# A fused attention, FFN and routed-expert kernel on one core: the two products of a Newton step on one pair of tiles, wider warm-up matmuls, and a new order of all engines up to the experts

## The chip, the cores and the metric

One NeuronCore of a Trainium2 chip runs the whole program in one launch. The metric is the device time of that launch in microseconds: lower is better. Below, TensorE (PE) is the matrix engine, VectorE (DVE), ScalarE (ACT) and GpSimd (POOL) are the elementwise engines, and SP is the queue that issues nearly all DMAs.

## The reference, cut to what matters

Three layers follow each other: Nyström attention over 4 batches, 8 heads, 576 positions and 64 dimensions; an FFN (512 to 2048 to 512) with elu on the 2304 tokens that result; and a layer of 8 experts of which each token takes two.

```python
q_lm, k_lm = means of q and k over 32 groups of 18 positions
A  = sm(q, k_lm)          # 576 x 32 for each batch and head; sm is a row softmax
Bm = sm(q_lm, k_lm)       # 32 x 32
C  = sm(q_lm, k)          # 32 x 576
Z = Bm.T / (norm1(Bm) * norminf(Bm) + 1e-06)
for _ in range(6):
    Z = 2 * Z - Z @ Bm @ Z
x = (A @ Z @ C @ v)       # heads side by side: 2304 x 512
h = x @ w_in
y = np.where(h > 0, h, np.exp(np.minimum(h, 0)) - 1) @ w_out
# routing: y @ w_gate + log1p(exp(y @ w_noise)) * noise, the two best of 8
# experts: out[tokens of e] += weight * (maximum(y @ w1[e], 0) @ w2[e])
```

## The kernel before, in words

**Attention**, one call of `attention(b)` for each batch. The 8 heads are two halves of four (`k.0`, `k.1`, `q.0`, `q.1`: loads of 0.59 MB). `lmmm` or `lmsum` sum the landmarks, by 9 products with an identity on TensorE (batch 0) or on VectorE or GpSimd (the others); `bmm` forms Bm's scores, `csmm` those of C, `asmm` those of A, and the functions beside them the softmaxes. The six Newton steps are written as R and Y: R begins as a difference from the identity, and each step squares it (`sqmm`, `sqout`) and adds the product of R and Y to Y (`umm`, `uout`). Each of these products is eight matmuls of 32 x 32 blocks in fp32, one for each head (`blocks`, L464). `sqout` copies R from PSUM on ScalarE, `uout` adds Y on VectorE. From Y, `cv` (the product of C with v), `zcv` and `zout` give Z, and `gmm` multiplies Z with the rows of w_in that belong to each head: that is G (512 columns for each call, four calls for a batch). So the FFN's first layer is one product of A with G.

**The FFN** runs over six chunks of tokens (512, 256, and four of 384) and 16 blocks of 128 hidden columns. For each, `l1` is the product of A and G, `X`, `T`, `S`, `H`, `O` are the steps of elu (`O` is the low half of the float16 pair, a subtraction on VectorE or GpSimd, by the letter behind the item), and `l2` adds the product with w_out's 16 pieces of 128 rows (`wout`). w_in's 16 pieces and w_out's 16 pieces arrive as 64-bit words and are put into floats first, by `I.j.0` to `I.j.3` and `Wa.k.0` to `Wa.k.3` (one on ScalarE, two on VectorE, one on GpSimd), and w_out is then split into a float16 pair (`Wb`).

**Routing and experts.** `RT` to `RS` choose the experts and write the rows; expert 0's steps and then experts 1 to 7 follow. The order of experts 1 to 7 is written in loops behind the table.

**What sets the order.** Nothing is scheduled by the compiler: `ORDER` is a string of items, and `do` calls for each item, in that order, the function that issues its instructions. Each engine then runs its own instructions in the order of the string, and SP its loads. An engine that stands in front of a wait stands with everything behind it. `0:sqmm.1` is step 1 of batch 0, `L2.3.5.1` block 5 of chunk 3 for its token tile 1, `wi.6` and `Wl.5` are loads of weight pieces, `F.16` is 16 warm-up matmuls (`warm`, L661), which compute nothing that is used. In batch 2 and 3 the products of both kinds, `pq` (R and R) and `pu` (R and Y), take turns in one PSUM bank ("n"), which is also that of chunk 0's fourth token tile. In batch 0 each has its part of a fixed bank.

Of the kernel before, what the change touches and what calls it, by code (L numbers as in the profile page):

```python
# [8 lines left out]
F32 = mybir.dt.float32  # L9
F16 = mybir.dt.float16  # L10
# [7 lines left out]
M = 32  # L18
# [38 lines left out]
I.3.0 I.6.3 I.4.1 Wa.0.1 0:asmm.0 F.16 F.16 I.4.2 Wl.5 I.2.3 I.5.1 0:xtl.1.1.0 0:astr.0 0:xth.1.1.1 0:lcp.0.A
0:xtl.1.1.1 wi.1 0:xtp.0.1.0 0:asmax.0 0:bmm I.5.2 Wl.1 0:csmm.0 I.4.3 0:bmax 0:xth.0.1.0 0:xtp.0.1.2 F.16 0:bex
0:csmax.0 wi.14 wi.7 I.3.3 0:assub.0.G 0:bnorm 0:nmm Wa.0.2 F.15 0:nval 0:csexp.0 Wa.1.0 Wa.5.0 Wb.4.0.V F.15
0:xth.1.1.2 Wa.1.1 0:sqmm.0 Wa.5.1 I.1.1 Wa.1.2 I.5.0 0:xtl.1.1.2 0:xtl.0.1.0 0:sqout.0 wi.10 0:xth.0.1.2 nz.3.1 Wa.5.2  # L60
0:y0 Wa.1.3 I.7.1 Wl.3 0:csmm.1 F.16 Wa.5.3 F.3 0:xtp.0.1.1 Wa.3.0 0:asexp.0 0:umm.0 0:sqmm.1 0:sqout.1 0:csmax.1
# [122 lines left out]
def attn_ffn_moe_kernel(ctx: ExitStack, tc: tile.TileContext, q: bass.AP, k: bass.AP, v: bass.AP,  # L184
# [1213 lines left out]
```

## Time and profile before

| | us |
|---|---|
| median of 3 runs | 792.57 |
| lowest and highest | 788.42, 794.16 |
| profiled execution, its own time | 790.42 |
| its span in the profile | 788.6 |

The span is what the views below divide. A view of stretches gives the busy time of each engine between two times; a timeline lists the instructions of one engine in order, with what it waited for ahead of each; groups by line sum the instructions of one source line. What the rows say, by the words of the profile: `L469` is line 469, `pq<-R` is a tile and what it is made from, `x16` the count of instructions or of instruction parts.

### The profile page before, as it was taken

The page shows a single profiled execution, that of the slowest core. Times are in us where ns is not written, and L with a number is a line of the kernel's source. Part 1 is how long each engine was busy: PE and PEld are TensorE (multiplying, and loading weights), DVE is VectorE, ACT ScalarE, POOL GpSimd, SP SyncE. Part 2 cuts the span into 40 slices and gives each one's busy share as a digit, 9 for nine tenths or more (in the row PEclk, how much of TensorE's full clock was granted, in tenths as well). Part 3 has the DMA queues.
Part 4 walks back from the last instruction along what each step waited for, and adds up shares of the span by engine and source line. Part 5 has one row for each costly group of instructions (what it writes and reads, how often), then busy time and mean ns, then how long its engine had stood idle before and what let it go on. Part 6 is the DMA issues. An engine that isn't in the chain of part 4 may idle for free. (4 is left out here: it accounts for less than half of the span.)

```text
span 788.6 us, 18639 instructions
## 1 busy us (share of the span) xinstructions
PE 762.4 (97%) x7517; PEld 454.8 (58%) x7518; DVE 623.5 (79%) x1366; ACT 426.9 (54%) x821; POOL 274.6 (35%) x303
## 2 busy tenths in 40 slices
PE   8878998999999999999999999999999999999997
PEld 8653444564544545665555775665747566574763
DVE  5969988797875777655737579989999998999951
ACT  3757776757556456446432365555636555564530
POOL 2434455636241332141403252333425132312222
PEclk9979999999999999999999999999999999999999
DMA  9977696286896221614242976474756647472381
GB/s 343 329 193 199 160 285 256 42 171 197 238 246 150 87 83 41 174 69 107 82 81 96 177 190 150 106 212 62 244 94 198 141 86 218 73 238 26 38 302 67
DMA packets 136205, 123.25 MB, mean 156 GB/s; under 512 B 102892, under 2 KB 105964, under 8 KB 136017
## 3 DMA queue, kind: packets, MB, share of 16 engines
q1 hardware_dynamic: 125392, 100.67, 45.6%
q0 software_dynamic: 10720, 21.34, 12.7%
q8 instruction: 60, 0.98, 0.5%
q14 instruction: 33, 0.26, 0.1%
HBM read 70.62 MB, written 39.76 MB: 140 GB/s over the span
## 5 line engine op out<-in xcount | busy, mean ns | idle before, releaser
L692 PE MATMUL y<-wout,g 128*128 128x512 f16 x864 | 208.2, 382 | 2.1 <-issue 1.9
L1135 PE MATMUL ey<-w,eh 128*128 128x512 f16 x768 | 167.2, 379 | 0.0
L1161 POOL DMA_INDIRECT acc<-eo,tk x35 | 73.8, 2108 | 207.6 <-ACT eo L219 78.8
L692 PEld LDWEIGHTS <-g 128*128 128x128 f16 x864 | 80.0, 98 | 92.5 <-issue 10.2
L1135 PEld LDWEIGHTS <-eh 128*128 128x128 f16 x768 | 75.0, 98 | 89.1
L654 PE MATMUL h<-AT,G 128*128 128x192 f16 (+3 forms) x768 | 108.7, 288 | 3.4 <-DVE e L680 3.3
L654 PEld LDWEIGHTS <-G 128*128 128x128 f16 x768 | 63.7, 98 | 46.4 <-issue 11.6
L685 POOL TENSOR_TENSOR g<-e,g 128x384 f16<-128x384 f32 (+2 forms) x45 | 43.9, 976 | 132.4 <-ACT g L219 114.7
L219 ACT ACTIVATE eh<-c 128x300 f16<-128x300 f32 x112 | 47.8, 453 | 65.1 <-DVE c L1057 57.2
L219 ACT ACTIVATE g<-e 128x384 f16<-128x384 f32 (+2 forms) x96 | 49.2, 520 | 48.2 <-DVE e L680 23.2
L219 ACT ACTIVATE e<-h 128x384 f32<-128x384 f32 (+2 forms) x96 | 46.3, 486 | 40.4 <-PE h L654 23.3
L680 DVE SCALAR_TENSOR_TENSOR e<-e,h 128x384 f32<-128x384 f32 (+2 forms) x96 | 51.3, 546 | 14.6 <-ACT e L219 12.5
L219 ACT ACTIVATE eo<-ey,ws 128x512 f32<-128x512 f32 (+3 forms) x60 | 32.4, 540 | 45.7 <-PE ey L1135 33.6
L877 POOL DMA_INDIRECT xs<-rows,pos x36 | 37.7, 1048 | 54.3 <-DVE mcum L861 26.4
L916 DVE SCALAR_TENSOR_TENSOR w<-ew,w 128x1024 f16<-128x1024 f32 x36 | 43.9, 1242 | 13.7 <-ACT w L219 11.9
L1040 PE MATMUL eb<-tx,wpC 128*128 128x300 f16 x336 | 47.4, 291 | 0.0
L1069 DVE SCALAR_TENSOR_TENSOR eh<-c,eh 128x300 f16<-128x300 f32 x112 | 46.0, 461 | 1.0 <-ACT eh L219 0.2
L685 DVE TENSOR_TENSOR g<-e,g 128x384 f16<-128x384 f32 (+2 forms) x51 | 29.4, 581 | 19.0 <-ACT g L219 18.8
L1057 DVE TENSOR_TENSOR c<-eb,u 128x300 f32<-128x300 f32 x84 | 36.6, 459 | 3.6 <-PE eb L1040 3.6
L1040 PEld LDWEIGHTS <-wpD 128*128 128x128 f16 x336 | 32.8, 98 | 11.4 <-issue 1.3
L1040 PEld LDWEIGHTS <-wpB 128*128 128x128 f16 x336 | 32.9, 98 | 10.0
L1040 PEld LDWEIGHTS <-wpC 128*128 128x128 f16 x336 | 32.7, 97 | 10.1
(256 smaller groups left out, 1379.7 us busy)
## 6 DMA issues: line engine op xcount, KB each, us to landing
ew<-in_moe_w_dram SPq DMA_DIRECT2D x64, 512.0 KB
wi<-in_moe_w_in_dram SPq DMA_DIRECT2D x16, 512.0 KB
wo<-in_moe_w_out_dram SPq DMA_DIRECT2D x16, 512.0 KB
k<-in_k_dram SPq DMA_DIRECT2D x8, 576.0 KB
q<-in_q_dram SPq DMA_DIRECT2D x8, 576.0 KB
v<-in_v_dram SPq DMA_DIRECT2D x4, 1152.0 KB
out_dram<-acc SPq DMA_DIRECT2D x1, 4608.0 KB
xs<-zrow SPq DMA_DIRECT2D x3, 1300.0 KB
```

The source lines that it names most:

```text
L219: return A.activation(o, i, f, **kw)
L654: T.matmul(p[:, c0:c0 + n], GT[b, f // 8][:, g, x, fs], AT[b][:, g, y, o:o + n], start=(i == 0), stop=(i == 5))
L680: V.scalar_tensor_tensor(x[1], x[1], x[2], x[0], op0=ALU.mult, op1=ALU.max)
L685: e.tensor_tensor(out=HT[c, f][:, 1], in0=x[1], in1=HT[c, f][:, 0], op=ALU.subtract)
L692: T.matmul(YP[c, t], h[:, x, 128 * t:128 * t + 128], WOUT[f][:, y], start=(f == 0 and i == 0), stop=(f == 15 and i == 2))
L877: n = nc.gpsimd.indirect_dma_start(out=xs[:, :], out_offset=bass.IndirectOffsetOnAxis(ap=R["pos"][:, i // 2, i % 2:i % 2 + 1], axis=0), in ...
L916: V.scalar_tensor_tensor(dst[1][:, ks, :], t, scale, dst[0][:, ks, :], op0=ALU.mult, op1=ALU.subtract)
L1040: T.matmul(p, w_op(e, w, s, k, f), x_op(e, x, t, k), start=(i == 0 and k == 0), stop=(i == 2 and k == 1))
L1057: V.tensor_tensor(out=o, in0=EB[n, f], in1=EU[a, f], op=ALU.add)
L1069: V.scalar_tensor_tensor(lo, o, 0.0, hi, op0=ALU.max, op1=ALU.subtract)
L1135: T.matmul(p, EH[e, f][:, x, 128 * j:128 * j + 128], W2T[e][y][:, f, :], start=start, stop=stop)
L1161: nc.gpsimd.indirect_dma_start(out=acc[:, :], out_offset=bass.IndirectOffsetOnAxis(ap=TK[e][:live(j), j:j + 1], axis=0), in_=EO[e, j], in_ ...
```

## The change

1. **Newton.** R and Y of a step stand side by side in one tile `R` of [128, 2, 2, 32] (head half, R or Y, columns). `nm(i)` multiplies R with [R|Y]: eight matmuls of 32 rows and 64 columns, whose result is the next R and the addend of the next Y. `sqmm` is left for the first step alone and `umm` for the last. A batch has 56 block matmuls in place of 96. `sqout(i + 1)` and `uout(i)` both read the result of `nm(i)`, and `nm(i + 1)` reads both of theirs.
2. **Warm-ups.** `warm` multiplies a tile of ones with itself up to four times side by side, so with up to 512 columns. 258 matmuls of 128 columns become 63 of at most 512 (239 times 128 columns).
3. **Names.** The big tiles of w_in, w_out and G are made by whichever of their parts the order names first, and so is C's row of sums.
4. **ORDER** is written anew up to the experts, SP's loads with it. 61 of the 96 `O` stand on GpSimd (45 before), 35 on VectorE (51 before); in chunk 0 VectorE has 3 of them (7 before). 60 `T` stand on ScalarE (56 before).

```diff
 ORDER = """
-wi.0 F.16 0:k.0 Wl.4 I.0.0 0:q.0 Wa.4.0 F.16 F.16 0:xtp.1.0.0 0:xtp.1.0.2 wi.2 I.0.1 0:xth.1.0.0 I.0.2 0:lmmm.1.0 Wa.4.1
+F.30 0:k.0 0:q.0 0:xtp.1.0.0 0:xtp.1.0.1 0:xth.1.0.1 Wl.4 0:xtp.1.0.2 0:xtp.0.0.1 0:q.1 0:xtp.0.0.2 0:lmmm.0.0
...
+    hot = cst.tile([128, 128], F16, name="hot")
+    V.memset(hot, 1.0)
...
-            if kk % 4 == 0:
-                t = half(f"wout{kk}").rearrange("p (k s f) -> p k s f", k=4, s=2)
+            if kk not in WOUT:
+                t = half(f"wout{kk // 4}").rearrange("p (k s f) -> p k s f", k=4, s=2)
...
+        def ry(i):
+            if i not in R:
+                R[i] = sa.tile([128, 2, 2, M], F32, tag="R", bufs=NR, name=f"R{b}{i}")
+            return R[i]
+
         def sqmm(i):
-            p = X["pq", i] = small(f"pq{b}{i}", n_tag, 0, 64).rearrange("p (g m) -> p g m", g=2)
-            x = X["BB"][:, 1] if i == 0 else R[i - 1]
-            blocks(p, x, x)
+            p = X["pq", 0] = small(f"pq{b}{i}", n_tag, 0, 64).rearrange("p (g m) -> p g m", g=2)
+            blocks(p, X["BB"][:, 1], X["BB"][:, 1])
+
+        def nm(i):
+            p = X["pq", i + 1] = small(f"pu{b}{i}", n_tag, 0, 128).rearrange("p (g s m) -> p g s m", g=2, s=2)
+            blocks(p, R[i][:, :, 0], R[i])
...
-                act(r, p)
+                act(r, p[:, :, 0])
...
         def umm(i):
             p = X["pu"] = small(f"pu{b}{i}", u_tag, 256, 64, "l1").rearrange("p (g m) -> p g m", g=2)
-            blocks(p, R[i], X["Y"])
+            blocks(p, R[i][:, :, 0], R[i][:, :, 1])

         def uout(i):
-            Y, X["Y"] = X["Y"], tile_a([128, 2, M], "Y", 2)
-            V.tensor_tensor(out=X["Y"], in0=X["pu"], in1=Y, op=ALU.add)
+            p, o = (X["pq", i + 1][:, :, 1], ry(i + 1)[:, :, 1]) if i < 5 else (X["pu"], tile_a([128, 2, M], "Y"))
+            V.tensor_tensor(out=o, in0=p, in1=R[i][:, :, 1], op=ALU.add)
+            X["Y"] = o
...
-        for _ in range(n):
-            T.matmul(WARM[0][:, :128], ident16, ident16, start=True, stop=True)
+        while n:
+            w = min(n, 4)
+            T.matmul(WARM[0][:, :128 * w], hot, hot[:, None, :].to_broadcast([128, w, 128]), start=True, stop=True)
+            n -= w
```

**SP's queue, the start of the program.** `k01` is k of batch 0, its second half; `wi` and `wo` are raw pieces of w_in and w_out, `noise_t` the routing's noise. Before:

```order
L1211 DMA wi00_114<-in_moe_w_in_dram 128x1024
L228 DMA k00_133<-in_k_dram 128x1152
L267 DMA wo4_135<-in_moe_w_out_dram 128x1024
L228 DMA q00_139<-in_q_dram 128x1152
L1211 DMA wi02_183<-in_moe_w_in_dram 128x1024
L228 DMA q01_212<-in_q_dram 128x1152
L1211 DMA wi12_216<-in_moe_w_in_dram 128x1024
L228 DMA k01_223<-in_k_dram 128x1152
```

And now:

```order
L226 DMA k00_125<-in_k_dram 128x1152
L226 DMA q00_127<-in_q_dram 128x1152
L267 DMA wo4_139<-in_moe_w_out_dram 128x1024
L226 DMA q01_149<-in_q_dram 128x1152
L737 DMA noise_t_97<-in_moe2_noise_dram 32x4x8
L226 DMA k01_187<-in_k_dram 128x1152
L1224 DMA wi01_212<-in_moe_w_in_dram 128x1024
L267 DMA wo5_218<-in_moe_w_out_dram 128x1024
```

k's second half is the sixth load in place of the eighth, behind two weight pieces fewer; `v0`, batch 0's v, is the 21st load in place of the 27th.

**TensorE, the Newton steps of batch 2.** `pu2i` and `pq2i` are the PSUM results of step i, `R2i` and `Y2` its operands, `y22` and `g2_f` result and left operand of the FFN's second layer, `pcv2` the product with v. Before:

```order
L469 MATMUL pu23_3509<-Y2_3416,R23_3468 32x32 x8
L692 LDWEIGHTS g2_8_3425
L692 MATMUL y22_3048<-wout8_1561,g2_8_3425 128x512
L692 LDWEIGHTS g2_8_3425
L692 MATMUL y22_3048<-wout8_1561,g2_8_3425 128x512
L692 LDWEIGHTS g2_8_3425
L692 MATMUL y22_3048<-wout8_1561,g2_8_3425 128x512
L469 MATMUL pq25_3523<-R24_3503 32x32 x8
```

And now:

```order
L469 MATMUL pu20_2950<-R20_2900 32x64 x8
L704 LDWEIGHTS g2_5_2731
L704 MATMUL y22_2740<-wout1_205,g2_5_2731 128x512
L704 LDWEIGHTS g2_5_2731
L704 MATMUL y22_2740<-wout1_205,g2_5_2731 128x512
L704 LDWEIGHTS g2_5_2731
L704 MATMUL y22_2740<-wout1_205,g2_5_2731 128x512
L469 MATMUL pu21_2969<-R21_2959 32x64 x8
L534 MATMUL pcv2_2980<-v2_1839,ET20_2860 32x64 x8
```

Two narrow groups, of R and Y and of R alone, stood for each step, with FFN products between them; now one group of 64 columns stands for each, which reads one tile, and between steps 0 and 1 lie three FFN products.

**GpSimd, chunk 0.** `g0_f` is the low half of the FFN's activations of chunk 0, `wo` and `wout` are w_out's pieces, `lmt211` and `k12` are the partial and the whole sum of batch 2's k, second half. Before:

```order
L685 TENSOR_TENSOR g0_10_1724<-e0_10_1683,g0_10_1724 128x512
L263 TENSOR_TENSOR wo10_1516<-wo10_1516 128x512
L263 TENSOR_TENSOR wo13_1461<-wo13_1461 128x512
L292 TENSOR_TENSOR wout12_1777<-wo12_1387,wout12_1777 128x512
L263 TENSOR_TENSOR wo11_1544<-wo11_1544 128x512
L292 TENSOR_TENSOR wout8_1561<-wo11_1544,wout8_1561 128x512
L685 TENSOR_TENSOR g0_12_1916<-e0_12_1843,g0_12_1916 128x512
```

And now:

```order
L697 TENSOR_TENSOR g0_11_1456<-e0_11_1358,g0_11_1456 128x512
L263 TENSOR_TENSOR wo11_1289<-wo11_1289 128x512
L697 TENSOR_TENSOR g0_10_1510<-e0_10_1379,g0_10_1510 128x512
L326 TENSOR_TENSOR lmt211_1595<-k21_1451 128x576
L328 TENSOR_TENSOR lmt211_1595<-lmt211_1595 128x256
L328 TENSOR_TENSOR lmt211_1595<-lmt211_1595 128x128
L328 TENSOR_TENSOR lmt211_1595<-lmt211_1595 128x64
L329 TENSOR_TENSOR k12_1592<-lmt211_1595 128x64
L292 TENSOR_TENSOR wout2_1278<-wo11_1289,wout2_1278 128x512
L263 TENSOR_TENSOR wo12_1389<-wo12_1389 128x512
L263 TENSOR_TENSOR wo13_1360<-wo13_1360 128x512
```

The sum of batch 2's k stands now between two subtractions of chunk 0 and the pieces 2, 12 and 13 of w_out; before it stood in chunk 1.

## Rows read from the trace of the kernel before

**Rows 1.** The page, busy time and instructions of each engine over the whole execution.

```profile
PE 762.4 (97%) x7517; PEld 454.8 (58%) x7518; DVE 623.5 (79%) x1366; ACT 426.9 (54%) x821; POOL 274.6 (35%) x303
```

**Rows 2.** Busy time in four stretches; the columns are named in its line.

```profile
core 0: us, PE busy (x) PEld busy (x) DVE busy (x) ACT busy (x) POOL busy (x), PEclk, DMA share, GB/s
0.00:58.10 58.10, 46.20 (x820) 39.69 (x822) 41.83 (x114) 31.27 (x67) 20.50 (x25) 0.91 0.88 293
58.10:140.00 81.90, 76.49 (x780) 32.85 (x777) 74.38 (x144) 60.31 (x118) 42.07 (x40) 0.96 0.71 217
140.00:406.40 266.40, 263.39 (x2603) 141.61 (x2596) 187.67 (x520) 150.37 (x331) 91.48 (x129) 1.00 0.49 129
406.40:788.60 382.20, 376.35 (x3327) 240.67 (x3325) 319.58 (x592) 184.94 (x307) 120.56 (x111) 1.00 0.59 142
```

**Rows 3.** TensorE's timeline, prologue; start, us, engine line op, [idle before <- releaser].

```profile
16.46 2.27 PE L336 MATMUL l1b<-k,ident 128*128 128x128 f32 x18 [0.77 <-DMA k<-in_k_dram]
...
24.48 0.27 PE L430 MATMUL nb<-lT 64*32 64x32 f16 x15
...
29.66 0.33 PE L469 MATMUL nb<-BB 32*32 32x32 f32 x16
...
43.90 0.18 PE L469 MATMUL l1b<-Y,R 32*32 32x32 f32 x1 [2.63 <-issue]
...
46.32 2.79 PE L524 MATMUL pcv<-v,ET 96*32 96x64 f32 x96 [1.36 <-DMA v<-in_v_dram]
...
51.36 0.70 PE L558 MATMUL l1b<-Yd,CV 128*64 128x64 f32 x8
51.99 2.53 PE L666 MATMUL warm<-ident 128*128 128x128 f16 x22
...
56.10 2.18 PE L666 MATMUL warm<-ident 128*128 128x128 f16 x36
58.12 3.18 PE L654 MATMUL h<-AT,G 128*128 128x512 f16 x12
61.23 1.09 PE L621 MATMUL pg<-win,Z 64*32 64x512 f32 x16
```

**Rows 4.** ScalarE's timeline, first loaded weight piece (same columns).

```profile
5.00 0.68 ACT L219 ACTIVATE wi<-wi 128x512 int32<-128x512 uint32 x1 [2.86 <-DMA wi<-in_moe_w_in_dram]
```

**Rows 5.** Busy time in the first 30 us (columns as in rows 2).

```profile
0.00:30.00 30.00, 25.55 (x353) 24.22 (x355) 20.48 (x64) 15.03 (x32) 8.51 (x14) 1.00 0.93 341
```

**Rows 6.** Groups by line, whole execution: busy us, mean ns | idle before.

```profile
L685 POOL TENSOR_TENSOR g<-e,g 128x384 f16<-128x384 f32 (+2 forms) x45 | 43.9, 976 | 132.4 <-ACT g L219 114.7 <-DVE sm L446 9.3 <-DVE ax L572 5.3
...
L685 DVE TENSOR_TENSOR g<-e,g 128x384 f16<-128x384 f32 (+2 forms) x51 | 29.4, 581 | 19.0 <-ACT g L219 18.8
...
L323 DVE TENSOR_REDUCE k<-q 128x64 f32<-128x1152 f32 x5 | 10.7, 2144 | 0.0
...
L219 ACT ACTIVATE ET<-pe 96x512 f32<-96x512 f32 x12 | 6.9, 581 | 1.1 <-PE pe L511 1.1
...
L219 ACT ACTIVATE ax<-ax 128x576 f32<-128x576 f32 x8 | 5.4, 678 | 0.0
```

**Rows 7.** ScalarE's timeline, two copies of a Newton step, batch 0.

```profile
33.73 0.22 ACT L219 ACTIVATE R<-nb 128x64 f32<-128x64 f32 x1 [1.35 <-PE nb L469]
34.40 0.22 ACT L219 ACTIVATE R<-nb 128x64 f32<-128x64 f32 x1 [0.45 <-PE nb L469]
```

**Rows 8.** TensorE's timeline in batch 2's Newton steps and its product with v.

```profile
203.14 2.76 PE L692 MATMUL y<-wout,g 128*128 128x512 f16 x12
205.84 0.33 PE L469 MATMUL pq<-R 32*32 32x32 f32 x16
206.10 0.82 PE L692 MATMUL y<-wout,g 128*128 128x512 f16 x3
206.76 1.14 PE L654 MATMUL h<-AT,G 128*128 128x384 f16 x6
...
213.12 1.55 PE L524 MATMUL pcv<-v,ET 96*32 96x64 f32 x96
```

**Rows 9.** The page, VectorE's busy tenths in 40 slices of 19.7 us.

```profile
DVE  5969988797875777655737579989999998999951
```

**Rows 10.** Waits of SP's queue: us in total, times, longest us.

```profile
SPq L228 <- DVE wout L294: 10.4, 1, 10.4
```

More of the change, by code (lines that the diff above doesn't have):

```diff
@@ L57 @@
[L57 to L61, printed above, removed]
@@ new lines @@
+I.8.2 I.11.0 I.11.1 H.0.3 T.0.2.A O.0.3.G nz.0.3 S.0.2 L2.0.3.3 Wb.2.0.V X.0.4 1:xtr.0.0 Wa.6.0 L2.0.1.2 T.0.4.A
+Wb.2.1.V L2.0.1.1 H.0.2 L2.0.3.0 1:k.1 Wa.6.2 1:ltr.0 L1.0.7 Wa.7.0 S.0.4 I.10.1 O.0.2.G H.0.4 Wb.5.1.V O.0.4.G I.9.2
+I.15.1 L1.0.5 X.0.5 Wa.6.3 1:lcp.0.A T.0.5.A Wb.6.0.V 1:k.0 I.15.0 I.11.2 1:lmsum.1.0.V I.9.3 I.10.2 L2.0.4.3 Wa.7.1
+I.11.3 Wb.6.1.V I.10.3 I.8.3 nz.0.1 nz.3.0 Wl.8 L2.0.2.3 nz.1.3 S.0.5 L2.0.2.2 L2.0.2.1 1:xhi.1.0 1:v X.0.7 L2.0.3.1
+Wa.8.1 1:xlo.1.0 L2.0.4.2 Wa.7.2 T.0.7.A L2.0.4.0 Wa.8.0 L2.0.4.1 nz.0.0 H.0.5 O.0.5.G S.0.7 1:xhi.1.1 L1.0.6 0:gmm.2
@@ new lines @@
+1:asmm.1 L1.0.13 1:astr.1 O.0.11.G Wa.13.0 1:nm.1 Wa.11.3 X.0.12 Wa.12.1 1:sqout.2 L2.0.9.2 O.0.10.G Wb.10.1.V T.0.12.A
+fill.2 X.0.13 L2.0.10.2 1:uout.1 1:nm.2 1:sqout.3 Wa.12.2 2:lmsum.1.1.G S.0.12 L2.0.10.1 1:uout.2 Wb.11.0.G 1:nm.3
+H.0.12 Wa.14.1 2:q.1 1:sqout.4 Wa.15.0 T.0.13.A 1:asmax.1 Wa.13.1 1:cv Wb.11.1.G 1:uout.3 1:nm.4 1:assub.1.V 1:asmax.0
+1:sqout.5 O.0.12.V Wa.12.3 L2.0.11.1 1:cssum 1:asexp.1 L1.0.14 2:xhi.1.1 Wb.12.0.G 1:uout.4 1:cvout S.0.13 Wa.13.2
+1:assub.0.V 1:umm.5 1:uout.5 Wa.13.3 L2.0.10.0 1:asexp.0 Wb.13.0.V 1:assum.1 L2.0.10.3 Wb.12.1.G Wa.15.1 1:ybd.A
@@ new lines @@
+L2.5.0.2 H.5.3 L1.5.4 RT.4.1 S.5.1 H.5.1 RT.4.0 O.5.3.V L1.5.5 O.5.1.V X.5.4 X.5.5 L2.5.1.0 T.5.5.V L2.5.1.1 S.5.5
+T.5.4.A S.5.4 L2.5.1.2 L1.5.6 L1.5.7 H.5.4 P.0.1.1 WD.1.1.0 L2.5.2.2 O.5.4.G L2.5.2.0 L2.5.2.1 H.5.5 RG.4 L2.5.3.2
+L2.5.3.0 RA.4 L2.5.4.0 X.5.6 L2.5.3.1 L2.5.4.1 RB.4 T.5.6.A O.5.5.V L2.5.5.1 RC.4 X.5.7 T.5.7.A S.5.7 RD.4 S.5.6
+L2.5.4.2 H.5.6 RE.4 H.5.7 O.5.7.V RK.4 L1.5.8 O.5.6.V X.5.8 L1.5.9 T.5.8.A L2.5.5.0 RF.4 L2.5.6.1 X.5.9 L2.5.5.2
+L2.5.6.0 L2.5.6.2 T.5.9.V S.5.8 H.5.8 PD.1.7 L2.5.7.1 S.5.9 O.5.8.G L1.5.10 L2.5.7.2 H.5.9 L2.5.7.0 WD.1.0.1 X.5.10
@@ L172 @@
+T.5.14.A O.5.12.G L2.5.11.0 L2.5.12.1 S.5.14 H.5.14 X.5.15 L2.5.12.0 O.5.14.G T.5.15.V L2.5.12.2 L2.5.13.1 S.5.15 H.5.15
 L2.5.14.1 O.5.15.V L2.5.15.1 LX.0.0 L2.5.13.0 L2.5.13.2 YA.5.1 L2.5.14.0 L2.5.15.0 YA.5.0 YV.5.1 L2.5.14.2 L2.5.15.2
@@ L497, in csexp @@
             p, mx = X["pc", g], X["mx", g]
-            if g == 0:
+            if "cs" not in X:
                 X["cs"] = tile_a([128, 2, 2], "cs")
@@ L537, in y0 @@
         def y0():
-            X["Y"] = tile_a([128, 2, M], "Y", 2)
-            V.tensor_tensor(out=X["Y"], in0=X["BB"][:, 0], in1=X["sm"][:, 8:10, None].to_broadcast([128, 2, M]),
+            V.tensor_tensor(out=ry(0)[:, :, 1], in0=X["BB"][:, 0], in1=X["sm"][:, 8:10, None].to_broadcast([128, 2, M]),
                             op=ALU.mult)
@@ L613, in gmm @@
         def gmm(fb):
-            if fb % 2 == 0:
-                GT[b, fb // 2] = half(f"G{b}{fb}").rearrange("p (g s f) -> p g s f", g=2, s=2)
+            if (b, fb // 2) not in GT:
+                GT[b, fb // 2] = half(f"G{b}{fb // 2}").rearrange("p (g s f) -> p g s f", g=2, s=2)
             p = X["pg"] = [s1(f"pg{b}{fb}{g}", "a") for g in range(2)]
@@ L1206, in load_wi @@
         fb, kk = divmod(j, 4)
-        if kk % 2 == 0:
-            h = half(f"wi{fb}{kk}").bitcast(I32).rearrange("p (k n) -> p k n", k=2)
-            WI[j], WI[j + 1] = h[:, 0], h[:, 1]
+        if j not in WI:
+            h = half(f"wi{fb}{kk // 2}").bitcast(I32).rearrange("p (k n) -> p k n", k=2)
+            for i in range(2):
+                WI[j // 2 * 2 + i] = h[:, i]
         t = WI[j]
```

215 lines of the change are left out of this document (101 added, 114 removed).

## Prediction, made before the changed kernel was run

> **What bounds the kernel now.** Read first the engines' busy time [rows 1] and the stretches [rows 2]. TensorE is busy for 762.4 of 788.6 us. So a microsecond of its work is a microsecond of the whole, except where TensorE itself waits. Cut at the first product of the FFN's first layer (58.1) and at the first product of expert 0 (406.4), the stretches show where it waits. In the prologue (0 to 58.1) it is busy for 46.2, some 12 idle, and much of the busy time is warm-up. In the main stage (58.1 to 406.4) it idles for 5.4 of the first 81.9 and 3.0 of the other 266.4: 8.4 in 348.3. The experts' 382.2 are full, and nothing of them changes. The clock is below its full level in the first two stretches alone (0.91, 0.96).
>
> Then TensorE's own timeline of the prologue [rows 3]. Its last input of batch 0, k's second half, is there at 16.46; the matrix Bm is formed at 24.48; the first block product is at 29.66; at 43.90, near the end of the last ones, TensorE has stood for 2.63; the product with v waits until v lands at 46.3. From there to the first FFN product at 58.12 are 11.8 us, with 22 and then 36 warm-ups. The lower clock shows in the first of these: 22 matmuls of 128 columns in 2.53 are 115 ns each, the 1.2 GHz level. The prologue is a chain (load, Newton, v, G), and its length is what the new order can change.
>
> **The change part by part.**
>
> *Loads.* SP's queue decides when k01 and v land. The rate comes from two landings: the first 0.52 MB (a w_in piece) at 5.0 [rows 4], and k01, eighth in the queue with 4.46 MB through it, at 16.46 [rows 3]: 3.94 MB in 11.5 us, 0.344 MB/us. In the new queue 2.88 MB go through k01, so it lands at 5.0 + 2.36/0.344 = 11.9, which is 4.6 earlier. Before v stand 12.9 MB now and 9.7 in the new queue; with v itself 14.0 and 10.9. By 30 us 10.2 MB had moved, 341 GB/s [rows 5], so v would land at 32 to 36 and no longer be last.
>
> *Prologue chain.* From k01 to Bm are 8.0 now. The new order puts one more sum of 2.1 [rows 6] and the first scores between them, and has 16 warm-ups fewer: I take 9.3, so Bm at 21.2. From Bm to the first block product are 5.2 now, with 30 warm-ups ahead of it; in the new order the product comes ahead of the norms and I take 3.5: 24.7. From there to the first fused product are again 3.5 (norms, y0 and R on VectorE), then five steps. A bare step, from one R to the next, is 34.40 - 33.73 = 0.67 [rows 7]; but VectorE's new order has up to 2 us of weight conversions between two steps, so I take 2.0: the last product is at 24.7 + 3.5 + 10 = 38.2. v is there. Then, at the full clock: v's product 1.5 [rows 8], ten warm-ups (33 times 128 columns) 1.8 at 512/2.4 = 213 ns for 512 columns, Z 1.0 (its product is 0.70 at the lower level [rows 3], so about 0.35, and copy and hand-overs are an estimate), G's product 1.1 [rows 3], thirteen warm-ups 2.8: 46.4. I add 1.6 for waits behind conversions: the FFN begins at 48 instead of 58.1, **-10.1**. From below VectorE bounds it: of its 41.8 us before 58.1 [rows 2] about 37 stay ahead of that point (two sums and a few halves of conversions go behind it). In its first 19.7 us it is half idle [rows 9]; with loads 4.6 earlier I leave 7 idle: not under 44. From above: 58.1, no gain.
>
> *Newton.* Each step loses a group of eight block products on TensorE. By the starts a group takes 0.26 (205.84 to 206.10 [rows 8]). The twelve L2 products ahead of it take 2.70, where twelve times 213 ns are 2.56: with the changeover up to 0.40. I take 0.37. In batches 1 to 3, where TensorE is full, 5 groups x 3 x 0.37 = 5.5 go, **-5.5**, if a group 64 columns wide costs what one of 32 does. The nearest row of that kind is v's product: fp32, 64 columns wide, tiles of 32 columns side by side, 96 instructions in 1.55, 16 ns each; the 16 of a Newton group take 0.26, also 16 ns each [rows 8]. So I take no extra cost. The other end is twice 0.26.
>
> The Trainium skill, TensorE: Matmul & The Clock Gate, section "Step-by-step: what each phase is for", says the opposite: throughput is purely N cycles for N columns. By that rule 64 columns take twice what 32 do. No row here has both widths of one product; v's row speaks for 16 ns per instruction and not for columns. It is rival B.
>
> *The wait that it adds.* A fused product needs both copies of the step before, R from ScalarE and Y from VectorE, and behind it on TensorE everything stands in line. It is hidden where the order gives TensorE other work for longer than 0.67 plus what is queued on the two engines. In batch 2 only three L2 products (0.66 [rows 8]) lie between the first two steps, with up to two activations of the kind of 0.58 and 0.68 [rows 6] ahead of R; in batch 1 the new order has one pair as close. Two or three such places of 0.3 to 0.9: **+2**, bounds 0 and 15 x 1.3 = 20 (every step).
>
> *Warm-ups.* 258 matmuls of 128 columns become 63 of up to 512 (239 x 128 columns in all). Per column they are the same; 195 pairs of instructions go. All stand ahead of the FFN and are in the chain above.
>
> *Order of the main stage.* 16 subtractions of the FFN's low halves go from VectorE (581 ns) to GpSimd (976 ns) [rows 6]: -9.3 on VectorE, +15.6 on GpSimd, which is busy 42 of 82 and 91 of 266 [rows 2]. VectorE is busy 74.4 of 81.9 from 58.1 to 140; about 4.5 more of its work falls there (41.8 - 37.3) and 4 of the subtractions x 0.58 = 2.3 less, so it stays just under TensorE's own time. The idle 8.4 of TensorE I leave as it is (0 to 25), since the order of every stall is new: **0**.
>
> **The sum.** 48 + (348.3 - 5.5 + 2 = 344.8) + 382.2 = 775.0. The profiled execution took 790.4 for a span of 788.6, so 1.8 more: 776.8, or 13.6 less. The median of the runs, 792.6, is 2.2 above the profiled one; I allow for half of it: **778**. Without the waits and with the chain at its shortest it would be 44 + 342.8 + 382.2 + 1.8 = 770.8; with no gain in the prologue 786.9, by the runs 788.
>
> **The rivals.**
>
> A. *The head start is given back.* The FFN begins 10 us earlier with fewer conversions done, and VectorE, at 91% between 58.1 and 140 [rows 2], sets the pace there: each weight row that is late holds L2. For it: that 91%. Against it: subtractions go to GpSimd, and VectorE is idle for 16 us of the prologue. Price: 8 of the 10.1 are lost: 778 + 8 = 786.
>
> B. *Columns count.* The fused group costs 0.26 more: 5 x 3 x 0.26 = 3.9 come back: 782. Against it: v's row.
>
> C. *GpSimd held by a load; slower.* The kernel sums batch 2's k on GpSimd in the middle of chunk 0, right behind subtractions and ahead of four weight rows. GpSimd goes in order, so it stands until that k has landed. SP has held one load of q or k for 10.4 us behind a buffer [rows 10]. GpSimd makes five such sums for batches 2 and 3; if three of them stand 10.4 each and L2 stands with them, 31 come on: 809. It passes the kernel before from some 14 us of added waiting and is 1% slower from 22. Against it: a hold of that length stands once in this trace, and conversions are buffered some rows ahead.
>
> D. *More than the chain.* TensorE at full clock through the prologue and half of the 8.4 idle gone, with the chain at 45: 45 + (342.8 - 4.2) + 382.2 + 1.8 = 767.6; with the median's offset 769.
>
> **How the numbers follow.** Forecast 0.50, A 0.15, B 0.10, C 0.08, D 0.15, and 0.02 that the new queues cost as much as they bring. A measurement of this kernel tells about 1% from no change: 784.6 and 800.5. Under 784.6 lie 0.95 of the forecast's half, all of D, most of B and a quarter of A: 0.47 + 0.15 + 0.08 + 0.04, which I round down to 0.73. Over 800.5 lie most of C and a little of the rest: 0.07. Between: 0.20. The range takes in D nearly to its time, A and B whole and a prologue without gain, and leaves C out: 768 to 792.
>
> **What would show it.** Right: the first FFN product at 46 to 50; v's product without a wait for v; a fused group in batches 1 to 3 as long as a single one was (0.33 shown [rows 8]); expert 0 beginning at 390 to 396; the stretch behind it 382. Wrong: the first FFN product after 54, TensorE idle over 15 us between it and expert 0, or GpSimd waiting for k in chunk 0.

## The result, and the profile after: 1.1% slower

The changed kernel takes 798.92 us (median of 6 runs, 798.14 to 801.17), the kernel before 791.06 (6 runs, 788.42 to 794.16): a ratio of 1.0108, 95% interval 1.0077 to 1.0139. The forecast was 778, the range 768 to 792. Both are missed, and the direction too. The profiled execution took 801.01 us for a span of 799.2.

The page's busy times, against [rows 1]:

```profile
PE 757.5 (95%) x7002; PEld 440.9 (55%) x7003; DVE 641.2 (80%) x1347; ACT 430.9 (54%) x825; POOL 293.7 (37%) x319
```

TensorE has 4.9 us less to do and idles for 15.5 us more. VectorE, which has 16 subtractions fewer, is busy for 641.2 us in place of 623.5. 15.6 of GpSimd's 19.1 more were expected.

The stretches, cut where [rows 2] cut them: at the first FFN product (52.92), at 140 and at the first product of expert 0 (416.59); the columns are those of [rows 2]:

```profile
0.00:52.92 52.92, 40.91 (x545) 26.75 (x547) 43.47 (x108) 29.21 (x62) 18.04 (x22) 0.97 0.90 300
52.92:140.00 87.08, 73.69 (x675) 31.36 (x674) 85.96 (x138) 61.96 (x119) 52.59 (x50) 0.98 0.65 173
140.00:416.59 276.59, 267.09 (x2460) 142.09 (x2458) 192.21 (x512) 154.62 (x339) 102.41 (x138) 0.99 0.52 138
416.59:799.20 382.61, 375.82 (x3326) 240.71 (x3324) 319.52 (x592) 185.10 (x307) 120.67 (x111) 1.00 0.57 142
```

The prologue is 5.2 us shorter (52.92 against 58.12). The main stage takes 363.7 in place of 348.5 (58.12 to 406.65), the experts 382.6 in place of 382.0: -5.2 + 15.1 + 0.7 = 10.6, the difference of the spans. In the main stage TensorE is as busy as before (340.8 against 340.1) but idle for 22.9 us in place of 8.4. From 52.92 to 140 VectorE is busy for 85.96 of 87.08 us: it sets the pace there. Of the 14.5 us of idle time that came on, 8.0 lie before 140 (13.4 against 5.4) and 6.5 behind it. What TensorE waits for in the main stage, the five longest rows (us in total, times, longest):

```profile
PE h L664 <- DVE e L692: 7.7, 7, 2.5
PE pc L420 <- DVE ax L582: 1.9, 1, 1.9
PE pg L631 <- DVE G L639: 1.7, 1, 1.7
PE y L704 <- DVE wout L294: 1.3, 1, 1.3
PE pu L469 <- DVE R L557: 1.2, 3, 0.6
```

All rows of this view together put 18.9 of the 22.9 us down to VectorE. Why has VectorE more to do, with less on its list? Its groups by line, over the whole execution (busy us, mean ns of one), show it. Of the kernel before:

```profile
L262 DVE SCALAR_TENSOR_TENSOR wo<-wo,woc 128x512 int32<-128x512 int32 x16 | 11.6, 732 | 0.0
...
L262 DVE SCALAR_TENSOR_TENSOR wi<-wi,win 128x512 int32<-128x512 int32 x16 | 10.7, 685 | 0.1
...
L261 DVE TENSOR_SCALAR woc<-wo 128x512 int32<-128x512 int32 x16 | 7.0, 446 | 1.8 <-DMA wo<-in_moe_w_out_dram 1.8
...
L261 DVE TENSOR_SCALAR win<-wi 128x512 int32<-128x512 int32 x16 | 6.7, 421 | 5.6 <-DMA wi<-in_moe_w_in_dram 5.6
...
L352 DVE SCALAR_TENSOR_TENSOR lm<-k,lm 128x128 f16<-128x128 f32 x16 | 5.0, 353 | 0.1
```

And of the changed kernel:

```profile
L692 DVE SCALAR_TENSOR_TENSOR e<-e,h 128x384 f32<-128x384 f32 (+2 forms) x96 | 51.9, 549 | 24.1 <-ACT e L217 22.2 <-ACT gw L217 0.3
...
L262 DVE SCALAR_TENSOR_TENSOR wo<-wo,woc 128x512 int32<-128x512 int32 x16 | 15.2, 952 | 0.0
...
L262 DVE SCALAR_TENSOR_TENSOR wi<-wi,win 128x512 int32<-128x512 int32 x16 | 14.3, 901 | 0.0
...
L261 DVE TENSOR_SCALAR win<-wi 128x512 int32<-128x512 int32 x16 | 11.6, 733 | 0.0
...
L261 DVE TENSOR_SCALAR woc<-wo 128x512 int32<-128x512 int32 x16 | 9.7, 604 | 0.0
...
L352 DVE SCALAR_TENSOR_TENSOR lm<-k,lm 128x128 f16<-128x128 f32 x16 | 9.4, 626 | 1.2 <-ACT lm L217 1.2
```

Count and shape are the same, the mean is not: the two steps of a weight conversion went from 421 and 446 ns to 733 and 604, and from 685 and 732 to 901 and 952; a landmark's low half from 353 to 626. The middle one of each group of conversions lasts as before (about 420 and 690): the mean is raised by some that last up to 1.39 and 1.77 us. `e<-e,h`, which has one operand in PSUM (its 384-column form 547 before, 551 after), stayed as it was, and so did a transpose of 576 columns (770 and 772) and the landmark sum (2144 and 2184). Summed over all forms that both kernels have, instructions of the same form cost VectorE some 30 us more before the experts, and the moved subtractions took 9.4 away: its busy time before the first expert product went from 304.1 to 321.6 (neighbours overlap at their edges, so the durations of all instructions sum to 342.9 and 362.9 us). Where the time goes is seen when the two engines are read side by side, VectorE first, GpSimd second:

```profile
72.73 1.64 DVE L262 SCALAR_TENSOR_TENSOR wi<-wi,win 128x512 int32<-128x512 int32 x1
74.29 1.26 DVE L261 TENSOR_SCALAR win<-wi 128x512 int32<-128x512 int32 x1
75.47 1.52 DVE L262 SCALAR_TENSOR_TENSOR wi<-wi,win 128x512 int32<-128x512 int32 x1
...
79.00 0.69 DVE L262 SCALAR_TENSOR_TENSOR wi<-wi,win 128x512 int32<-128x512 int32 x1
...
92.14 2.38 DVE L352 SCALAR_TENSOR_TENSOR lm<-k,lm 128x128 f16<-128x128 f32 x2
```

```profile
72.30 1.53 POOL L697 TENSOR_TENSOR g<-e,g 128x512 f16<-128x512 f32 x1 [0.38 <-ACT g L217]
73.78 1.48 POOL L263 TENSOR_TENSOR wo<-wo 128x512 int32<-128x512 int32 x1
75.23 1.22 POOL L263 TENSOR_TENSOR win<-wi 128x512 int32<-128x512 int32 x1
77.07 1.04 POOL L263 TENSOR_TENSOR win<-wi 128x512 int32<-128x512 int32 x1 [0.63 <-DVE wi L262]
...
92.04 2.33 POOL L697 TENSOR_TENSOR g<-e,g 128x512 f16<-128x512 f32 x2 [5.43 <-ACT g L217]
```

The conversion steps at 72.73, 74.29 and 75.47 take 1.64, 1.26 and 1.52 us while GpSimd runs one two-operand instruction behind the other; at 79.00, with GpSimd idle, the same step takes 0.69. At 92.14 two instructions of together 0.49 take 2.38, and end with GpSimd's pair. So such an instruction of VectorE stands until GpSimd's is through. This is the mechanism that the prediction did not have; the experiments below test it. The Trainium skill, SBUF — State Buffer, section "Who interferes with whom", states a lock of this kind: VectorE and GpSimd share one pair of ports; an instruction of VectorE with two SBUF operands contends with one of GpSimd that reads SBUF, and one in a two-port mode has the pair, or waits for it, for a whole instruction. The rows agree, in the exceptions too (the PSUM operand, the reduction). In which mode the scalar step of the conversion (L261) runs, no run here shows.

### The profile page after: what moved, and what is told of

It is laid out like the page before. It is cut to its first block, busy times and chain, and to the rows that moved or that the text cites. A ratio compares the mean times of both kernels' runs of the same rounds, so it can differ in the third digit from the quotient of the medians.

```text
span 799.2 us, 17629 instructions
## 1 busy us (share of the span) xinstructions
PE 757.5 (95%) x7002; PEld 440.9 (55%) x7003; DVE 641.2 (80%) x1347; ACT 430.9 (54%) x825; POOL 293.7 (37%) x319
## 5 line engine op out<-in xcount | busy, mean ns | idle before, releaser
L697 POOL TENSOR_TENSOR g<-e,g 128x384 f16<-128x384 f32 (+2 forms) x61 | 61.3, 1007 | 161.9 <-ACT g L217 157.8
L664 PEld LDWEIGHTS <-G 128*128 128x128 f16 x768 | 63.8, 98 | 49.8 <-issue 13.1
L692 DVE SCALAR_TENSOR_TENSOR e<-e,h 128x384 f32<-128x384 f32 (+2 forms) x96 | 51.9, 549 | 24.1 <-ACT e L217 22.2
L928 DVE SCALAR_TENSOR_TENSOR w<-ew,w 128x1024 f16<-128x1024 f32 x36 | 43.2, 1221 | 12.7 <-ACT w L217 10.9
L1052 PEld LDWEIGHTS <-wpD 128*128 128x128 f16 x336 | 32.8, 98 | 12.2 <-issue 2.3
L1052 PEld LDWEIGHTS <-wpC 128*128 128x128 f16 x336 | 32.7, 97 | 10.1
L217 ACT ACTIVATE w<-ew 128x1024 f16<-128x1024 f32 x36 | 37.0, 1049 | 0.2
```

The costliest lines, as they stand in the source:

```text
L217: return A.activation(o, i, f, **kw)
L664: T.matmul(p[:, c0:c0 + n], GT[b, f // 8][:, g, x, fs], AT[b][:, g, y, o:o + n], start=(i == 0), stop=(i == 5))
L692: V.scalar_tensor_tensor(x[1], x[1], x[2], x[0], op0=ALU.mult, op1=ALU.max)
L697: e.tensor_tensor(out=HT[c, f][:, 1], in0=x[1], in1=HT[c, f][:, 0], op=ALU.subtract)
L928: V.scalar_tensor_tensor(dst[1][:, ks, :], t, scale, dst[0][:, ks, :], op0=ALU.mult, op1=ALU.subtract)
L1052: T.matmul(p, w_op(e, w, s, k, f), x_op(e, x, t, k), start=(i == 0 and k == 0), stop=(i == 2 and k == 1))
```

## The experiments

Theory S (sharing): the new order puts more of VectorE's two-operand work beside GpSimd's, each such instruction lasts up to GpSimd's end, and VectorE, already at its limit from the FFN's start to 140, holds TensorE. Rivals: Q, the new order makes its own waits whatever an instruction lasts; W, the fused product's wait for both copies; H, it is the hand-over from GpSimd that costs, not the sharing. Each ratio is to the kernel before in the same measurement, with its 95% interval; the measurements are from different chips, on which the kernel before takes 786.74 to 791.92, so ratios are compared and not times. "VectorE" is its busy time up to the first product of expert 0, "idle" TensorE's idle time in the main stage, both in us from the profile.

| kernel | median us | before us | ratio | VectorE | idle |
|---|---|---|---|---|---|
| before | | | 1 | 304.1 | 8.4 |
| after | 798.92 | 791.06 | 1.0108 (1.0077 to 1.0139) | 321.6 | 22.9 |
| after_noadd | 785.43 | 786.74 | 0.9982 (0.9967 to 0.9997) | 307.7 | 13.1 |
| before_noadd | 783.55 | 786.74 | 0.9964 (0.9947 to 0.9980) | 301.0 | 6.0 |
| after_o | 798.45 | 786.74 | 1.0142 (1.0116 to 1.0168) | 316.5 | 22.2 |
| before_nm | 783.59 | 786.74 | 0.9944 (0.9926 to 0.9961) | 305.7 | 8.3 |
| after_dummyadd | 797.88 | 790.35 | 1.0107 (1.0076 to 1.0138) | 316.7 | 22.2 |
| after_dummyset | 791.68 | 790.35 | 1.0009 (0.9991 to 1.0028) | 306.9 | 18.8 |
| after_split | 802.82 | 790.35 | 1.0170 (1.0146 to 1.0194) | 318.8 | 24.6 |
| before_nm_v | 787.68 | 790.35 | 0.9965 (0.9946 to 0.9983) | 305.2 | 9.5 |
| after_c0v | 798.04 | 790.19 | 1.0106 (1.0075 to 1.0136) | 317.8 | 22.1 |
| before_nm_c0v | 790.47 | 790.19 | 1.0000 (0.9978 to 1.0022) | 312.4 | 12.2 |
| before_nm_short | 781.49 | 790.19 | 0.9898 (0.9867 to 0.9929) | 301.6 | 8.3 |
| after_noadd_set | 781.61 | 791.92 | 0.9881 (0.9858 to 0.9905) | 299.4 | 10.1 |

**Without GpSimd's additions.**

```diff
-                lambda: V.scalar_tensor_tensor(hi, hi, -0x40000000, tmp, ...
-                lambda: G.tensor_tensor(out=hi if dst is None else dst, in0=hi, in1=lo, op=ALU.add)), ...
+                lambda: V.scalar_tensor_tensor(hi if dst is None else dst, hi, -0x40000000, tmp, ...
+                lambda: None), ...
```

> The changed kernel without GpSimd's 32 closing additions of the weight conversions (the last 3 bits of each weight are left out; VectorE writes the result at the same place). Theory S (sharing): VectorE's instructions last longer beside GpSimd's two-operand ones, and the new order puts more of them beside each other. Then the conversions are back at 0.42 and 0.69 us, VectorE's busy time before the experts falls from 321 to about 300, TensorE's idle time in the main stage from 23 to under 13, and the time to 785 to 789. Theory Q (order): the new order makes its own waits, however long an instruction takes. Then VectorE stays at 315 or more and the time at 795 to 798.

> The same left out of the kernel before (the last 3 bits of each weight). Theory S: there is less to win, since its conversions last 0.42 to 0.45 and 0.69 to 0.73 us now: 787 to 790, so that the changed kernel without the additions is level with it or ahead. Theory Q: it gains as much as the changed kernel, and the distance between the two stays at 8 us.

The changed kernel gains 1.3%, the kernel before 0.4%: of a distance of 1.1% some 0.2% are left, and there the intervals meet. VectorE falls by 13.9 in the one and by 3.1 in the other. So the loss against the kernel before hangs on these additions, as S has it and Q has not. The size of the fall was less than expected (307.7 and not 300), since VectorE's conversions in after_noadd are still long:

```profile
L262 DVE SCALAR_TENSOR_TENSOR wo<-wo,woc 128x512 int32<-128x512 int32 x16 | 13.7, 858 | 0.0
L262 DVE SCALAR_TENSOR_TENSOR win<-wi,win 128x512 int32<-128x512 int32 x16 | 12.9, 818 | 0.0
...
L261 DVE TENSOR_SCALAR win<-wi 128x512 int32<-128x512 int32 x16 | 9.6, 605 | 0.0
...
L352 DVE SCALAR_TENSOR_TENSOR lm<-k,lm 128x128 f16<-128x128 f32 x16 | 9.3, 623 | 1.2 <-ACT lm L217 1.2
...
L261 DVE TENSOR_SCALAR woc<-wo 128x512 int32<-128x512 int32 x16 | 7.8, 485 | 0.6 <-DMA wo<-in_moe_w_out_dram 0.6
```

The two are level, but the change was to be faster. Without the additions the prologue is 7.7 us shorter in the new order (51.72 against 59.38), and the main stage 7.9 longer (350.3 against 342.4): the whole head start is given back here too, and what the Newton product saves with it. Whether that is the sharing that is left, or VectorE that begins the stage with fewer conversions done (the prediction's rival A), these two runs do not part.

**The same load on GpSimd, but nobody waits for it.** In after_noadd, at each of the 32 places:

```diff
+                lambda: [G.tensor_tensor(out=idle_t, in0=ident, in1=onesbd, op=ALU.add) for _ in range(3)]), ...
```

and in the other kernel `[G.memset(idle_t, 0.0) for _ in range(7)]`.

> The changed kernel without the closing additions (as in after_noadd, the last 3 bits of each weight left out), but at each of their 32 places GpSimd adds two constant tiles of 128x128 three times (some 1.4 us) into a tile that nobody reads. Nobody waits for them. Theory S: they alone bring the lengthening of VectorE's instructions back, VectorE's busy time before the experts is 6 or more above after_noadd's and the time 5 to 10 us above it. Rival H (after_noadd gained because nothing had to wait for GpSimd's hand-over any more): within 2 us of after_noadd.

> The same with seven memsets of 128x128 in place of the three additions (some 1.4 us, GpSimd reads nothing). Theory S, if what VectorE waits for is GpSimd's reading of operands: within 2 us of after_noadd, VectorE's instructions not longer. If any work of GpSimd holds VectorE: as after_dummyadd.

VectorE's busy time is the third busy time of these rows, up to expert 0, of after_dummyadd first and after_dummyset second (columns as in [rows 2]):

```profile
0.00:414.07 414.07, 381.70 (x3678) 200.36 (x3680) 316.72 (x756) 245.37 (x518) 190.48 (x272) 0.98 0.60 167
```

```profile
0.00:408.60 408.60, 379.18 (x3678) 199.09 (x3680) 306.89 (x756) 244.81 (x518) 183.85 (x400) 0.99 0.61 169
```

Additions for which nobody waits bring back the whole loss: 0.9982 becomes 1.0107, and VectorE's busy time grows by 9 us. So it is not the hand-over: H falls. Memsets leave VectorE's busy time as it was (306.9 against 307.7) and cost 0.3%, 2 us. That they cost anything may be the price of GpSimd coming later to its other work. By the ratios it is about a quarter of what the additions cost (0.3% of 1.25%); by TensorE's idle time in the profiled executions it is more than half (5.7 of 9.1), so its size stays open. The pair isn't quite of one length (the additions took 57 us in all, the memsets 48), so a part of the 1% between them may be that as well.

**What was left.** In after_noadd, chunk 0's 13 subtractions on GpSimd are made memsets of the same tile:

```diff
+        if part == "O" and c == 0 and e is G:
+            for _ in range(3):
+                G.memset(HT[c, f][:, 1], 0.0)
-        if part == "O":
+        elif part == "O":
```

> after_noadd, and in chunk 0 GpSimd's 13 low-half subtractions (1.34 us each) are replaced by three memsets each of the same tile (some 1.3 us together; the low halves of these activations are left out). GpSimd is as long occupied and ScalarE, VectorE and TensorE wait for it as before, but it reads nothing there. Theory S: VectorE's conversions, which in after_noadd still took 0.60 and 0.82 to 0.86, come to under 0.5 and 0.75, its busy time before the experts falls by 5 to 9 from 308, and the time by 2 to 5 us (ratio to before 0.992 to 0.996): then what was left of the loss in after_noadd was sharing as well. If the rest is the order's own waits: within 1 us of after_noadd (0.997 to 1.000).

It gains another 1.0%, more than expected, and VectorE's busy time falls by 8.3, as expected, though the memsets took longer (39 in 22.2 us, against 17.4 for the 13 subtractions). VectorE's conversions of this kernel:

```profile
L262 DVE SCALAR_TENSOR_TENSOR wo<-wo,woc 128x512 int32<-128x512 int32 x16 | 12.1, 757 | 0.0
L262 DVE SCALAR_TENSOR_TENSOR win<-wi,win 128x512 int32<-128x512 int32 x16 | 11.8, 746 | 0.0
...
L261 DVE TENSOR_SCALAR win<-wi 128x512 int32<-128x512 int32 x16 | 7.9, 500 | 0.0
L261 DVE TENSOR_SCALAR woc<-wo 128x512 int32<-128x512 int32 x16 | 7.3, 457 | 0.8 <-DMA wo<-in_moe_w_out_dram 0.8
...
L352 DVE SCALAR_TENSOR_TENSOR lm<-k,lm 128x128 f16<-128x128 f32 x16 | 5.5, 384 | 1.2 <-ACT lm L217 1.2
```

So the subtractions on GpSimd held VectorE as the additions did. One thing goes beside it: a memset does not wait for ScalarE's high half as the subtraction does, so a part of this 1.0% may be that wait, and this run does not part them; the kernel before with the same edit was not tried. And the head start is not kept here either: VectorE has no more to do than in before_noadd (299.4 against 301.0), the prologue is 8.2 us shorter (51.21), and the main stage still 4.0 longer (346.4). So rival A may have a share of its own beside the sharing; that is not shown.

**Who does the subtractions.** In after_o each letter of an `O` is that of the order before; in after_c0v and before_nm_c0v, those of chunk 0 are all `V`.

```diff
-... O.0.0.G ... O.0.1.G ...
+... O.0.0.V ... O.0.1.V ...
```

> The changed kernel with each low-half subtraction of elu on the engine that it had before (46 change engine, 16 more on VectorE in the sum); all else stays. Theory S with the moved subtractions as the cause: GpSimd's busy time falls by 15, VectorE's total stays where it is although it has 9 us more to do, and the time is 791 to 795. Theory S with the place of the conversions as the cause: VectorE's total rises by about 9 and the time is 798 to 806. Theory Q: 797 to 801.

> The changed kernel with all 16 low-half subtractions of chunk 0 on VectorE (13 move there from GpSimd). On VectorE one takes 0.66 to 0.70, on GpSimd 1.39. Theory S: 18 us of GpSimd's two-operand work go, 8.8 of VectorE's own come, and the lengthening falls by 5 to 9, so VectorE's busy time before the experts stays at 318 to 325 and the time is within 4 us of the changed kernel's (ratio to before 1.006 to 1.016). Without sharing VectorE's 8.8 would come on top in the stretch where it is full: ratio 1.019 or more.

> before_nm with chunk 0's 9 subtractions of GpSimd on VectorE. There VectorE's conversions lie beside GpSimd's less often, so there is less to win back: 6.2 more on VectorE, 2 to 4 less lengthening, chunk 0 near VectorE's limit: 1 to 5 us above before_nm (ratio to before 0.996 to 1.001).

In after_c0v VectorE gets 13 subtractions, 8.8 us by the row of one, and its busy time falls by 3.9: 12.7 us of lengthening went with them, so in the changed order a subtraction on GpSimd costs VectorE at least as much as doing it. The time stays. In the order of before the same edit adds 6.7 to VectorE (9 x 0.69 = 6.2) and 0.6% to the time: there the subtractions on GpSimd lie where they hold nothing. after_o fits neither form of S whole. VectorE's busy time fell by 5.1, where no change or a rise was expected, and the time did not fall (1.0142 against 1.0108; the intervals meet). So the subtractions that were moved are not what makes the changed kernel slow: with every one back on its engine of before it is as slow. What is left is where the conversions and the rest of GpSimd's work stand beside each other in the new order. Nor does VectorE's total alone decide; which of the 46 letters holds whom was not followed up.

**The Newton product by itself.**

```diff
-            blocks(p, R[i][:, :, 0], R[i])
+            for s in range(2):
+                blocks(p[:, :, s], R[i][:, :, 0], R[i][:, :, s])
```

is after_split. before_nm is the changed kernel's code (so with the wider warm-ups too) with the order of before, in which each pair of `sqmm` and `umm` is put as one `nm`, with `sqout` and `uout` right behind it:

```diff
-... 0:umm.0 0:sqmm.1 0:sqout.1 0:csmax.1 0:uout.0 0:sqmm.2 0:sqout.2 ... 0:umm.1 ... 0:uout.1 ...
+... 0:nm.0 0:sqout.1 0:uout.0 0:csmax.1 0:nm.1 0:sqout.2 0:uout.1 ...
```

> The order of before with the changed Newton step and warm-ups: each fused product stands where the first of the two stood that could (or the second), the copies of R and Y right behind it. Theory S or Q: 15 groups of 0.26 less in batches 1 to 3, each of the others 0.1 longer, and 0 to 2 of new waits: 787 to 790. Theory W (the fused product's wait for both copies is what the change costs): 794 or more, with waits for R of several us on TensorE.

> The changed kernel with the fused product taken apart again: for each step eight matmuls of R and R and eight of R and Y, 32 columns each, one group behind the other, all else as it is. A group of 64 columns took 0.36 from start to start and two of 32 take 0.52: 15 x 0.16 = 2.4 in batches 1 to 3 and less than 1 in batch 0. So 2 to 4 us longer than the changed kernel (ratio to before 1.013 to 1.016). If the fused product is what the change costs (theory W), it is no longer or shorter.

The fused product is worth 0.56% in the order of before, together with the wider warm-ups, and 0.6% in the new one: 4.4 us (by the interval 3 to 6) and 4.9 (by the two intervals some 2 to 8). W falls. before_nm is faster than both kernels.

**Two more.** before_nm_v only moves the load of v:

```diff
-... wi.12 ... wi.8 ... Wl.7 ... wi.11 ... Wl.2 ... 0:v ...
+... 0:v wi.12 ... wi.8 ... Wl.7 ... wi.11 ... Wl.2 ...
```

> before_nm with the load of v five weight pieces earlier. TensorE waits there 1.70 for v, and 0.49 for what comes behind: up to 2 us less than before_nm if the prologue's chain sets it; if the pieces that now land 3 us later hold VectorE or ScalarE, which run in order, 0 to 3 us more.

It gains nothing over before_nm (0.9965 against 0.9944, intervals that meet), though TensorE waited 1.70 us there for v: what stands behind v in the queue is late in its place. The trace shows it: ScalarE stood 3.06 and 3.51 us for pieces of w_out that had not landed, ahead of copies of R (in before_nm 1.32 for the first and none for the second), TensorE then 1.91 and 2.46 for R and 2.27 for C transposed (`ET`), and the FFN began at 58.52 in place of 54.61.

before_nm_short is before_nm with after_noadd's edit, and ScalarE's step left out too:

```diff
-        return (lambda: act(lo, lo.bitcast(U32), scale=2.0 ** -29),
+        return (lambda: None,
```

> before_nm with a shorter conversion of the weights: the last 3 bits are left out, and with them ScalarE's first instruction and GpSimd's closing addition of each of the 32 pieces. before_noadd gained 0.36% on before, ScalarE's 21 us are mostly beside the path: 3 to 6 us under before_nm, ratio to before 0.987 to 0.991.

It is 1.0% faster than before. Of the kernels that keep the whole weights before_nm is the fastest, at 0.9944.

## Why the prediction was wrong

**Loads: right.** The sums of k01 on TensorE run without a wait for it from 13.03 (foretold: landed at 11.9), and v's product begins without waiting for v.

**Prologue chain: the mechanism right, the size half.** TensorE's timeline of the prologue, after (columns as in [rows 3]):

```profile
21.31 0.42 PE L430 MATMUL nb<-lT 64*32 64x32 f16 x24
...
25.49 0.33 PE L469 MATMUL nb<-BB 32*32 32x32 f32 x16 [2.42 <-DVE BB L450]
...
29.74 0.43 PE L469 MATMUL nb<-R 32*32 32x64 f32 x16 [1.02 <-DVE R L491]
...
41.00 0.33 PE L469 MATMUL l1b<-R 32*32 32x32 f32 x16 [0.67 <-DVE R L557]
...
44.27 0.53 PE L534 MATMUL pcv<-v,ET 96*32 96x64 f32 x21 [1.71 <-issue]
44.74 3.60 PE L677 MATMUL warm<-hot 128*128 128x384 f16 x10
...
52.92 2.75 PE L664 MATMUL h<-AT,G 128*128 128x512 f16 x12
```

Bm's scores were foretold for 21.2 and are at 21.31. Then it slips: the first block product at 25.49 (24.7), the first fused one at 29.74 (28.2), the last Newton product at 41.00 (38.2), the first FFN product at 52.92 (48). Of 10.1 us 5.2 came. VectorE, of which 37 us were reckoned ahead of the FFN, was busy for 43.47 there. The slip is partly the same sharing, in the chain itself: instructions of two columns, 0.17 alone, and one conversion step, 0.42 alone, on VectorE:

```profile
23.94 0.76 DVE L447 TENSOR_SCALAR sm<-sm 128x2 f32<-128x2 f32 x1
...
27.28 1.02 DVE L459 TENSOR_TENSOR sm<-sm 128x2 f32<-128x2 f32 x1
...
32.17 1.26 DVE L261 TENSOR_SCALAR win<-wi 128x512 int32<-128x512 int32 x1
```

The rest comes behind Newton. v's product stands for 1.71 in its middle, for which the profile names no releaser, and the ten warm-ups behind it take 3.60 where 1.8 was reckoned: 33 x 128 columns at 1.2 GHz are 3.52. The granted clock around them (columns as in [rows 2]):

```profile
36.00:41.00 5.00, 2.89 (x64) 1.19 (x61) 5.00 (x12) 2.19 (x6) 4.80 (x5) 1.00 1.02 350
41.00:44.27 3.27, 1.56 (x91) 1.36 (x92) 3.27 (x5) 2.39 (x5) 2.73 (x2) 1.00 1.08 309
44.27:48.30 4.03, 4.03 (x33) 1.70 (x32) 3.73 (x9) 0.71 (x2) 1.16 (x1) 0.58 0.99 352
```

From 36 to 44.27 TensorE was busy for 4.45 of 8.27 us at the full clock; then it was granted 0.58, which is mostly the lower level.

**Newton, -5.5: the sign right, the size less by the rows.** A fused group takes 0.35 from its start to the next (214.99 to 215.34), one of 32 columns 0.26 [rows 8]:

```profile
214.99 0.43 PE L469 MATMUL pu<-R 32*32 32x64 f32 x16
215.34 0.82 PE L704 MATMUL y<-wout,g 128*128 128x512 f16 x3
216.52 0.43 PE L469 MATMUL pu<-R 32*32 32x64 f32 x16 [0.35 <-ACT R L217]
216.87 1.55 PE L534 MATMUL pcv<-v,ET 96*32 96x64 f32 x96
```

So neither end of the bound: 22 ns per instruction, not 16 and not 32. Of rival B's 3.9 us 15 x 0.09 = 1.4 came. A group that went gave 0.26 back and the one that stayed took 0.09 more, so the rows give 15 x 0.17 = 2.6 us where 5.5 were reckoned; the 0.11 of changeover in the prediction's 0.37 stands in no row of its own. The runs give more, 4.9 in the new order and 4.4 in that of before, with the intervals above, and the second has in it a prologue that is 3.5 us shorter (54.61 against 58.12). What the rest is was not parted. The rule that was weighed, twice as long for twice the columns, does not hold for groups this small. **The added wait, +2: right in size.** TensorE's products of the steps waited 1.2 us for Y's sums in the main stage and 0.4 for R's copy, nearly all of it at 216.52.

**Order of the main stage, 0: this is the step that failed.** It said that VectorE loses 9.3 us, takes 4.5 from the prologue and so "stays just under TensorE's own time". Its own figures left no margin: 74.4 + 4.5 - 2.3 = 76.6 for VectorE, where TensorE was busy for 76.5 [rows 2]. The 9.3 were right as a sum over the moved instructions (9.4). But the instructions that stayed became some 30 us longer, because GpSimd's work now ran beside them (by after_o not the moved subtractions themselves), and VectorE's busy time up to the experts rose by 17.5 where a fall of 9.3 was reckoned. A mean duration from one order was used as if it belonged to the instruction; it belongs to the instruction and to what GpSimd does meanwhile. Then VectorE, at 91% of the stretch before [rows 2], had no room: it came to 98.7%, and TensorE's idle time grew by 14.5 to 22.9, past the 15 us that the prediction had named as a sign of being wrong. The 8.0 of the growth before 140 lie in rival A's place and on its engine. But A's price was bounded by the head start (8 of 10.1), with no reason for such a bound: an engine that sets the pace gives back as much as it is late. The bound of 0 to 25 for the idle time held the 22.9 that came, but the range was then made without its upper part.

**Rival C** did not come: GpSimd waited 16.2 us for ScalarE's high halves from 52.92 to 140 and for no k there.

The sum as it was measured: prologue -5.2, TensorE's idle time in the main stage +14.5, its busy time there +0.7 and the experts +0.7, which is +10.6 before rounding. That the busy time did not fall by the Newton groups' 2.6 is partly the clock: the same instructions of TensorE took 337.2 us in after_noadd, at a granted clock of 1.00 in the main stage, and 340.8 here, at 0.99 (0.98 from 52.92 to 140). What remains is not followed up.

## What to carry to other kernels

Before moving work from VectorE to GpSimd, or changing what stands beside what, look in the trace at what VectorE does beside GpSimd: in these runs an instruction with a PSUM operand, a reduction or a transpose kept its time, and one with two SBUF operands or a simple scalar step over SBUF waited for GpSimd's end. The same 32 additions on GpSimd were worth 0.4% in one order and 1.3% in the other, so an order of instructions is to be costed with durations that depend on the neighbour, and an engine at 91% of a stretch is a bound, not a reserve. A change of two parts is to be taken apart: here the product was worth 0.6%, and the new order around it cost 1.7% (after_split), nearly three times that.

## What the runs showed of the hardware that was not expected

A VectorE instruction on two columns, 0.17 us alone, took 1.02 beside GpSimd (at 27.28): what it loses is what is left of GpSimd's instruction, whatever its own size. Memsets on GpSimd did not lengthen VectorE's busy time up to the experts (306.9 us against 307.7 without them), additions of nearly the same length did (316.7). And a group of 16 fp32 instructions of 32 rows cost 0.26 us at 32 columns and 0.35 at 64.
